# Attention stage of a three-stage kernel: row copies out of PSUM, and a small addition, moved from VectorE to ScalarE

## The chip, the cores and the metric

The kernel runs on one core of one Trainium2 chip. The metric is the device time of one execution in microseconds; the time of a kernel is the median of several runs. Five engines work side by side, each through its own list of instructions in order: TensorE (PE in the rows; PEld is its weight load), VectorE (DVE), ScalarE (ACT), GpSimd (POOL) and SyncE (SP), which issues most transfers. They wait for one another by semaphores. TensorE writes its results to PSUM, a small memory of eight banks, from which VectorE and ScalarE read.

## What is computed

Three stages follow one another. Attention runs over 4 batches, 8 heads, 576 positions and 64 dimensions, with a window of 32 keys (dilated by 4 in the upper four heads). Its output, as 2304 rows of 512, goes through a mixture of 8 experts of which each row uses the one with the largest gate, and then through a dense two-layer block. Cut to what the change touches:

```python
scores = where(mask, scale * q @ k.T, -1e9)
attn = exp(scores - max(scores)); attn = attn / (sum(attn) + 1e-9)
x = (attn @ v).transpose(0, 2, 1, 3).reshape(2304, 512)
logits = x @ w_gate + modality_bias[modality_id]
e_idx = argmax(logits)
probs = exp(logits - max(logits)); probs /= sum(probs) + 1e-9
out[row] = probs[row, e_idx] * (relu(x @ w1[e_idx]) @ w2[e_idx])
```

The dense block comes after that and is not touched.

## The kernel before

The attention stage handles 16 pairs (batch b, head pair hp), in two halves each: a half, called a unit, is 5 or 4 blocks of 64 queries. The function attention() writes out a software pipeline by hand, as a loop over steps s = 0 to 37. The instructions of an engine run in the order in which this loop writes them. In step s it writes, in this order:

- on even s, the score matmuls of the pair s/2 (L1178 the mask, L1188 the scores; both units of the pair);
- emit_max_exp of unit s: the row maximum nb on VectorE (L1195), its scaling on ScalarE (L1196), 5 or 4 exponentials on ScalarE (L1200), each with a sum into su, and the addition of 1e-9 to su on ScalarE (L1202);
- emit_norm of unit s-1: a reciprocal on VectorE (L1209), and the multiplication on GpSimd (L1210);
- emit_b of unit s-3: transposes on TensorE (L1217), and the copy pt out of PSUM on VectorE (L1219);
- one store of rows that an earlier step made ready (L1301, by SyncE);
- emit_rows, where a pair of rows is pending (below);
- emit_c of unit s-4: the product with v on TensorE (L1232) and, after the second half, the copy xy on ScalarE (L1238, or L1240 with a stride for the dilated heads);
- routing work for the experts, on VectorE for the most part (from step 14 on; lines 240 to 360), loads of expert weights, and, in steps 19, 21, 23, 25, 27, 29, 33 and 35, the split of a weight tile: a cast whi on ScalarE (L201), then wlo on GpSimd (L203).

emit_rows(b, c, t0) turns the finished columns of xy into rows. It takes up to three tiles of 128 rows: one matmul each against [identity, gate weights] (L1252) writes 128 row values and 8 gate logits to the PSUM bank ps_r, of which there is one. For the first three head pairs of a batch (c < 3), the rows are copied to xc (L1255) and the logits to lp (L1256), both on VectorE; xc goes to memory by a store. For the last head pair the logits are added up first (L1267), and the rows are copied to xe (L1272 on VectorE, for the last batch L1270 on ScalarE). The next call of emit_rows, one step later, writes the same bank again. The rows of a pair i are made in steps 2i+6 and 2i+7: batch 0 in steps 6 to 13, batch 1 in 14 to 21, batch 2 in 22 to 29, batch 3 in 30 to 37.

emit_gate runs once for each batch, after its last rows (steps 13, 21, 29 and 37): a maximum, a subtraction, an exponential on ScalarE (L1289), the position of the maximum, the sum sg (L1294), the addition of 1e-9 (L1295) and a reciprocal (L1296), all on VectorE but the exponential.

After step 37 the experts and the dense block follow; the expert work already starts in steps 28 to 36 (gathered rows: L626, L635, L637; first layer: L644, L654, L655).

Of the kernel before, what the change touches and what calls it, by code (L numbers as in the profile page):

```python
# [17 lines left out]
ACTF = mybir.ActivationFunctionType  # L18
ALU = mybir.AluOpType
# [1072 lines left out]
def attention(tc, qT, kT, vW, mod, w_gate, m_bias, cs, msk, xy, oh, tri16, one16, x_dram, banks, w, moe, rt):  # L1092
    nc = tc.nc
    ident = cs[:, C_ID:C_ID + 128]
    scale = 1.0 / float(D) ** 0.5
    with ExitStack() as st:
# [149 lines left out]
        def emit_rows(b, c, t0):  # L1246
            g = groups[b]
            n = min(3, g.stop - t0)
            o = t0 - g.start
            r = banks.r[:, 0:3 * 136].rearrange("p (t e) -> p t e", e=136)  # L1250
            for t in range(n):
                nc.tensor.matmul(r[:, t, :], xy[:, c, (t0 + t) * 128:(t0 + t + 1) * 128], rw[:, c, :], start=True, stop=True)  # L1252
            if c < HP - 1:
                xc = xc_p.tile([128, 3, 128], F32, tag="xc", name="xc")
                nc.vector.tensor_copy(xc[:, 0:n, :], r[:, 0:n, 0:128])  # L1255
                nc.vector.tensor_copy(lp[:, o:o + n, c, :], r[:, 0:n, 128:136])  # L1256
                stores.append((t0, n, c, xc[:, 0:n, :], 128))
                if c == HP - 2 and t0 + n == g.stop:
                    m = len(g)
                    nc.vector.tensor_reduce(ls[:, 0:m, :], lp[:, 0:m].rearrange("p t c e -> p t e c"), axis=AX.X, op=ALU.add)  # L1260
                    nc.vector.tensor_tensor(ls[:, 0:m, :], ls[:, 0:m, :], bm[:, g.start:g.stop, :], op=ALU.add)
                return
            if t0 == g.start:
                xe_t[b] = xe_p.tile([128, 5, 144], F32, tag="xe", name="xe")
                nc.vector.memset(xe_t[b][:, :, 129:144], 0.0)
            xe = xe_t[b]
            nc.vector.tensor_tensor(ls[:, o:o + n, :], ls[:, o:o + n, :], r[:, 0:n, 128:136], op=ALU.add)  # L1267
            last = t0 + n == g.stop
            if b == B - 1:
                nc.scalar.copy(xe[:, o:o + n, 0:128], r[:, 0:n, 0:128])  # L1270
            else:
                nc.vector.tensor_copy(xe[:, o:o + n, 0:128], r[:, 0:n, 0:128])  # L1272
            if last:
                xe_t.pop(b)
                emit_gate(b, xe)
                stores.append((g.start, len(g), c, xe[:, 0:len(g), :], 144))

        def emit_gate(b, xe):
            g = groups[b]
            n = len(g)  # L1280
            sl = slice(g.start, g.stop)
            l = ls[:, 0:n, :]
            x = sm.tile([128, 5, E], F32, tag="x", name="x")[:, 0:n, :]
            mx = sm.tile([128, 5], F32, tag="mx", name="mx")[:, 0:n]
            sg = sm.tile([128, 5], F32, tag="sg", name="sg")[:, 0:n]
            bc = [128, n, E]
            nc.vector.tensor_reduce(mx, l, axis=AX.X, op=ALU.max)
            nc.vector.tensor_tensor(l, l, mx.unsqueeze(2).to_broadcast(bc), op=ALU.subtract)
            nc.scalar.activation(x, l, ACTF.Exp)  # L1289
            rev = cs[:, C_REV:C_REV + E].unsqueeze(1).to_broadcast(bc)  # L1290
            nc.vector.scalar_tensor_tensor(l, l, 0.0, rev, op0=ALU.is_equal, op1=ALU.mult)
            nc.vector.tensor_reduce(mx, l, axis=AX.X, op=ALU.max)
            nc.vector.tensor_tensor(oh[:, sl, :], rev, mx.unsqueeze(2).to_broadcast(bc), op=ALU.is_equal)
            nc.vector.tensor_reduce(sg, x, axis=AX.X, op=ALU.add)  # L1294
            nc.vector.tensor_scalar(sg, sg, 1e-9, None, op0=ALU.add)  # L1295
            nc.vector.reciprocal(xe[:, 0:n, 128], sg)  # L1296

        def emit_store():
# [4 lines left out]
        for s in range(NU + 6):  # L1303
# [16 lines left out]
            if pend:  # L1320
                emit_rows(*pend.pop(0))
            if s == 28:
                next(ids)
            if 0 <= s - 4 < NU:
# [3 lines left out]
                if half == 1:  # L1328
# [3 lines left out]
                    b, hp = pairs[i]  # L1332
# [295 lines left out]
```

## Time and profile before

| | |
|---|---|
| time, median of 3 runs | 771.34 us (769.26 to 773.08) |
| the profiled execution | 769.39 us |
| its span in the trace | 767.6 us |
| TensorE busy | 739.3 us, 96% |
| VectorE busy | 491.3 us, 64% |
| ScalarE busy | 387.4 us, 50% |
| GpSimd busy | 99.3 us, 13% |

The attention stage fills the first 126 us or so of the span; the score matmuls of step 14 start at 46.02 us, those of step 16 at 52.06, of step 22 at 69.92, of step 30 at 98.30. Times in the rows are microseconds from the span's start. A row of the timeline gives start, duration, engine, line, operation, what it writes and reads, and, in brackets, how long the engine stood idle before it and which instruction ended that. Instructions of one engine overlap a little at their ends, so the next one may start some 0.1 us before the last has ended.

### The profile page before, as it was taken

To read this page: it belongs to the slowest core of one execution; us is meant where nothing else is said; L and a number is where in the kernel's file an instruction comes from. 1 tells how busy PE (TensorE), PEld (TensorE's weight loads), DVE (VectorE), ACT (ScalarE), POOL (GpSimd) and SP (SyncE) were. 2 spreads that over 40 slices of the span, in tenths; PEclk is the share of its full clock that TensorE was granted. 3 is DMA by queue.
4 is the path that set the end of the run, shared out by engine and by line. 5 is a ranking of instruction groups with operands and counts; after the bars stand their busy time and mean duration, and the time that the engine had idled before them with its cause. 6 is when DMAs were issued, how large, how long until landed. Compare 5 with 4: busy or idle time off the path is not lost. (4 is left out here: it accounts for less than half of the span.)

```text
span 767.6 us, 15236 instructions
## 1 busy us (share of the span) xinstructions
PE 739.3 (96%) x5537; PEld 658.5 (86%) x5539; DVE 491.3 (64%) x1149; ACT 387.4 (50%) x1008; POOL 99.3 (13%) x99
## 2 busy tenths in 40 slices
PE   8999879999999999999799999999999999999996
PEld 4888669988998899889799889888889888988895
DVE  3678886773887878986487777864444464344341
ACT  4878753223323323442376666775445566454453
POOL 3325542230110100000000000011000003000003
PEclk9999999999999999999999999999999999999999
DMA  7789951269898967932257777488544556455512
GB/s 205 201 234 296 268 174 44 59 186 331 292 324 275 336 193 253 318 115 75 80 183 286 275 266 284 164 298 304 192 151 163 219 219 227 159 198 216 190 55 82
DMA packets 66189, 161.05 MB, mean 210 GB/s; under 512 B 8416, under 2 KB 25824, under 8 KB 60080
## 3 DMA queue, kind: packets, MB, share of 16 engines
q1 hardware_dynamic: 62592, 148.58, 57.0%
q0 software_dynamic: 3360, 11.01, 4.3%
q8 instruction: 49, 0.80, 0.4%
q14 instruction: 44, 0.36, 0.1%
q10 hardware_dynamic: 144, 0.29, 0.1%
HBM read 118.82 MB, written 41.04 MB: 208 GB/s over the span
## 5 line engine op out<-in xcount | busy, mean ns | idle before, releaser
L1439 DVE SCALAR_TENSOR_TENSOR t<-x,t 128x384 f32<-128x384 f32 x92 | 51.4, 558 | 80.0 <-ACT t L1432 79.8
L1462 PE MATMUL d_o<-d_ob,gh 128*128 128x512 f32 x288 | 89.6, 392 | 0.0
L1462 PE MATMUL d_o<-d_plain,gh 128*128 128x512 f32 x288 | 89.6, 392 | 0.0
L644 PE MATMUL ps_e<-hh,whi 128*128 128x256 f32 x288 | 82.9, 288 | 2.0 <-PEq L668 0.9
L644 PE MATMUL ps_e<-hl,whi 128*128 128x256 f32 x288 | 81.1, 282 | 0.0
L644 PE MATMUL ps_e<-hh,wlo 128*128 128x256 f32 x288 | 81.1, 281 | 0.0
L1431 ACT ACTIVATE t<-x 128x384 f32<-128x384 f32 x92 | 48.3, 525 | 52.5 <-DVE x L1452 52.5
L1447 DVE TENSOR_TENSOR gl<-t,gh 128x384 fp32r<-128x384 f32 x96 | 53.2, 554 | 17.8 <-ACT gh L1440 15.7
L1440 ACT CAST gh<-t 128x384 fp32r<-128x384 f32 x96 | 49.4, 514 | 29.6 <-DVE t L1439 29.3
L1452 DVE TENSOR_TENSOR x<-d_y,d_u 128x384 f32<-128x384 f32 x46 | 25.5, 554 | 53.1 <-ACT d_u L1543 53.1
L1462 PEld LDWEIGHTS d_o<-d_plain,gh 128*128 128x128 f32 x288 | 52.9, 188 | 6.1
L1462 PEld LDWEIGHTS d_o<-d_ob,gh 128*128 128x128 f32 x288 | 52.8, 188 | 5.7
L644 PEld LDWEIGHTS ps_e<-hh,whi 128*128 128x128 f32 x288 | 54.5, 189 | 3.1 <-issue 2.3
L1462 PE MATMUL d_o<-d_ob,gl 128*128 128x512 f32 x144 | 57.2, 397 | 0.0
L1462 PE MATMUL d_o<-d_plain,gl 128*128 128x512 f32 x144 | 57.1, 396 | 0.0
L1543 ACT COPY d_u<-d_x 128x384 f32<-128x384 f32 x46 | 22.0, 479 | 65.1 <-PE d_x L1419 65.1
L644 PEld LDWEIGHTS ps_e<-hh,wlo 128*128 128x128 f32 x288 | 54.5, 189 | 0.0
L644 PEld LDWEIGHTS ps_e<-hl,whi 128*128 128x128 f32 x288 | 54.4, 189 | 0.0
L663 ACT COPY xy<-ps_e 128x256 f32 (+1 forms) x36 | 13.4, 373 | 79.6 <-PE ps_e L644 65.1
L1432 ACT ACTIVATE t<-t 128x384 f32<-128x384 f32 x96 | 50.5, 526 | 3.0
L1471 POOL DMA_INDIRECT out<-o,pid x18 | 17.9, 995 | 248.4 <-ACT o L1470 246.6
L1200 ACT ACTIVATE p<-ps_s,nb 128x96 f32<-128x96 f32 x144 | 47.1, 341 | 2.7 <-issue 0.4
(441 smaller groups left out, 1922.8 us busy)
## 6 DMA issues: line engine op xcount, KB each, us to landing
raw<-in_w SPq DMA_DIRECT2D x48, 512.0 KB, 7.1
d_ab<-cache SPq DMA_DIRECT2D x15, 1024.0 KB, 6.2
d_ab<-cache SPq DMA_DIRECT2D x15, 768.0 KB, 4.3
r<-in_w_in SPq DMA_DIRECT2D x16, 512.0 KB, 5.8
r<-in_w_out SPq DMA_DIRECT2D x16, 512.0 KB, 5.4
wsc<-cva SPq DMA_DIRECT2D x32, 256.0 KB, 4.2
cache<-d_ab SPq DMA_DIRECT2D x8, 1024.0 KB, 5.0
d_ob<-cache SPq DMA_DIRECT2D x8, 1024.0 KB, 7.5
```

The source lines that it names most:

```text
L644: self.tc.nc.tensor.matmul(ps, a, b, start=(i == 0 and j == 0), stop=(i == n - 1 and j == 2))
L663: nc.scalar.copy(self.xy[:, d, off], ps)
L1200: nc.scalar.activation(p[:, j, :], s[:, j, :], ACTF.Exp, scale=scale, bias=nb[:, j:j + 1], accum_out=su[:, j:j + 1])
L1431: nc.scalar.activation(b.t, x, ACTF.Relu, scale=0.5, bias=0.5)
L1432: nc.scalar.activation(b.t, b.t, ACTF.Square)
L1439: nc.vector.scalar_tensor_tensor(b.t, x, 1.0, b.t, op0=ALU.max, op1=ALU.min)
L1440: nc.scalar.copy(b.h, b.t)
L1447: nc.vector.tensor_tensor(b.l, b.t, b.h.bitcast(F32), op=sub)
L1452: nc.vector.tensor_tensor(x, bank, other, op=add)
L1462: nc.tensor.matmul(po[i], a[:, q], o[:, x, f, :], start=(first and j == 0), stop=(last and j == 2))
L1471: nc.gpsimd.indirect_dma_start(out=outs[n][:, :], out_offset=bass.IndirectOffsetOnAxis(ap=pid[:, n:n + 1], axis=0), in_=t, in_offset=None)
L1543: nc.scalar.copy(part[("p1", "u2", "u3")[j // 2]], bank)
```

## The change

The copy of the rows to xc goes to ScalarE for batches 1, 2 and 3, and stays on VectorE for batch 0. The copy of the logits to lp stays where it is. The addition of 1e-9 to the gate's sum goes from VectorE to ScalarE, as an activation with a bias, in all four batches.

```diff
@@ emit_rows
             if c < HP - 1:
                 xc = xc_p.tile([128, 3, 128], F32, tag="xc", name="xc")
-                nc.vector.tensor_copy(xc[:, 0:n, :], r[:, 0:n, 0:128])
+                (nc.vector.tensor_copy if b < 1 else nc.scalar.copy)(xc[:, 0:n, :], r[:, 0:n, 0:128])
                 nc.vector.tensor_copy(lp[:, o:o + n, c, :], r[:, 0:n, 128:136])
@@ emit_gate
             nc.vector.tensor_reduce(sg, x, axis=AX.X, op=ALU.add)
-            nc.vector.tensor_scalar(sg, sg, 1e-9, None, op0=ALU.add)
+            nc.scalar.activation(sg, sg, ACTF.Copy, bias=1e-9)
             nc.vector.reciprocal(xe[:, 0:n, 128], sg)
```

In all, 18 copies (two in each of nine pairs of steps: nine of 128x384, six of 128x256, three of 128x128) and four additions change engines. The instructions of TensorE, GpSimd and SyncE stand in the same order as before.

On ScalarE, in step 16, the copy stands behind the exponentials and the su addition of unit 16 and ahead of the scaling of unit 17 (in brackets: the engines and transfer queues that an instruction waits for):

```order
 L1200 ACTIVATE p,su<-ps_s_82,nb 128x96 x4
 L1202 ACTIVATE su<-su 128x5 [waits Activation_49]
+L1255 COPY xc<-ps_r 128x384 [waits DMAHW1_49,DMAHW0_49,PE_49]
 L1196 ACTIVATE nb<-nb 128x4 [waits DVE_49]
-L1200 ACTIVATE p,su<-ps_s_83,nb 128x96 [waits PE_49,Activation_49,Pool_49]
+L1200 ACTIVATE p,su<-ps_s_83,nb 128x96 [waits Activation_49,Pool_49]
 L1200 ACTIVATE p,su<-ps_s_83,nb 128x96 x3
```

One instruction came in; the rest kept its order.

On VectorE, in the same step, between the maximum of unit 16 (L1195) and the routing work (L302, L303), with the reciprocal of unit 15 (L1209) and the pt copy of unit 13 (L1219):

```order
 L300 CAST ri<-rt_sm 1x1 [waits DVE_49]
 L1195 TENSOR_REDUCE nb<-ps_s_82 128x5 [waits PE_49]
-L1209 RECIPROCAL su<-su 128x4 [waits Activation_49,Pool_49]
+L1209 RECIPROCAL su<-su 128x4 [waits Pool_49]
 L1219 COPY pt<-ps_t 96x512 [waits PE_49]
-L1255 COPY xc<-ps_r 128x384 [waits DMAHW0_49,PE_49]
-L1256 COPY lp<-ps_r 128x3x8
+L1256 COPY lp<-ps_r 128x3x8 [waits Activation_49]
 L302 TENSOR_SCALAR rt_key<-cs,rt_r_138 128x8
 L303 TENSOR_SCALAR rt_k_143<-rt_key 128x8 [waits DVE_49]
```

The xc copy left the list, the lp copy got a wait for ScalarE, and the reciprocal lost one.

On ScalarE, in step 21, between the gate's exponential (L1289) and the xy copy of that step (L1238), with the weight cast (L201) behind it:

```order
 L1202 ACTIVATE su<-su 128x4 [waits Activation_49]
 L1289 ACTIVATE x<-ls 128x40 [waits DVE_49]
+L1295 ACTIVATE sg<-sg 128x5 [waits DVE_49]
 L1238 COPY xy<-ps_o 128x576 [waits PE_49]
 L201 CAST whi_97<-raw 128x1024 [waits DMAHW4_49]
```

The addition came in between, with a wait for VectorE.

## Rows read from the trace of the kernel before

**Rows 1.** The page's first part: busy time of each engine.

```profile
PE 739.3 (96%) x5537; PEld 658.5 (86%) x5539; DVE 491.3 (64%) x1149; ACT 387.4 (50%) x1008; POOL 99.3 (13%) x99
```

**Rows 2.** Windows: length; busy PE, PEld, DVE, ACT, POOL; clock; DMA share; GB/s.

```profile
46.02:57.98 11.96, 11.96 (x192) 10.21 (x191) 10.40 (x43) 8.81 (x47) 3.82 (x5) 1.00 0.84 237
...
81.58:98.30 16.72, 12.17 (x193) 10.14 (x192) 14.17 (x42) 11.54 (x49) 9.14 (x8) 1.00 0.79 231
...
110.00:126.00 16.00, 15.93 (x183) 15.02 (x182) 10.11 (x36) 7.61 (x13) 6.15 (x3) 1.00 0.38 112
```

**Rows 3.** Timeline of steps 16 and 17, three engines.

```profile
52.06 1.75 PE L1188 MATMUL ps_s<-k,q 64*64 64x96 f32 x36
...
53.85 0.66 DVE L1195 TENSOR_REDUCE nb<-ps_s 128x5 f32<-128x480 f32 x1 [0.28 <-PE ps_s L1188]
...
54.55 0.21 ACT L1196 ACTIVATE nb<-nb 128x5 f32<-128x5 f32 x1 [0.89 <-DVE nb L1195]
...
55.12 0.56 DVE L1255 COPY xc<-ps_r 128x384 f32<-128x384 f32 x1
...
55.60 0.17 DVE L1256 COPY lp<-ps_r 128x24 f32<-128x24 f32 x1
...
56.34 0.63 PE L1252 MATMUL ps_r<-rw,xy 128*128 128x136 f32 x4
...
56.49 0.55 DVE L1195 TENSOR_REDUCE nb<-ps_s 128x4 f32<-128x384 f32 x1
56.59 0.21 ACT L1202 ACTIVATE su<-su 128x5 f32<-128x5 f32 x1
...
57.08 0.20 ACT L1196 ACTIVATE nb<-nb 128x4 f32<-128x4 f32 x1 [0.28 <-DVE nb L1195]
...
58.09 0.16 DVE L1256 COPY lp<-ps_r 128x16 f32<-128x16 f32 x1
...
58.79 0.17 DVE L253 TENSOR_TENSOR rt_lo<-rt_rank,rt_tmp 128x4 f32<-128x4 f32 x1
58.80 0.20 ACT L1202 ACTIVATE su<-su 128x4 f32<-128x4 f32 x1
...
59.77 0.66 DVE L1195 TENSOR_REDUCE nb<-ps_s 128x5 f32<-128x480 f32 x1 [0.82 <-PE ps_s L1188]
```

**Rows 4.** Timeline of steps 36 and 37: the xe copies on ScalarE.

```profile
123.23 0.48 ACT L1270 COPY xe<-ps_r 128x384 f32<-128x384 f32 x1 [0.61 <-DVE ls L1267]
...
124.95 0.37 ACT L1270 COPY xe<-ps_r 128x256 f32<-128x256 f32 x1 [0.57 <-DVE ls L1267]
```

**Rows 5.** Timeline of steps 21 and 22: the gate's sum, and the next scaling.

```profile
71.59 0.19 DVE L1294 TENSOR_REDUCE sg<-x 128x5 f32<-128x40 f32 x1
...
72.78 0.21 ACT L1196 ACTIVATE nb<-nb 128x5 f32<-128x5 f32 x1 [0.33 <-DVE nb L1195]
```

**Rows 6.** Timeline of steps 24 to 28.

```profile
77.53 0.66 DVE L1195 TENSOR_REDUCE nb<-ps_s 128x5 f32<-128x480 f32 x1
...
79.51 1.86 DVE L327 TENSOR_TENSOR rt_v<-oh,rt_isM 128x72 f32<-128x72 bf16 x1
...
86.97 0.20 ACT L1196 ACTIVATE nb<-nb 128x5 f32<-128x5 f32 x1
...
94.03 0.20 ACT L1196 ACTIVATE nb<-nb 128x5 f32<-128x5 f32 x1
```

**Rows 7.** Timeline of steps 29 to 32, from the gate's addition on.

```profile
102.17 2.10 DVE L1295 TENSOR_SCALAR sg<-sg 128x4 f32<-128x4 f32 x1
...
105.06 0.21 ACT L1196 ACTIVATE nb<-nb 128x5 f32<-128x5 f32 x1 [3.26 <-DVE nb L1195]
...
105.83 1.27 PE L1217 MATMUL ps_t<-cs,p 128*96 128x128 f32 x5 [3.23 <-DVE pt L1219]
...
109.17 0.66 PE L635 MATMUL ps_s<-cs,xga 128*128 128x128 f32 x4
```

**Rows 8.** Windows, columns as in rows 2: the stretch behind that gap.

```profile
105.00:107.50 2.50, 1.67 (x8) 1.66 (x9) 1.79 (x7) 2.24 (x14) 0.83 (x1) 0.63 0.55 165
```

## The prediction

> **What bounds the kernel now.** I read the page's first part, then the table of windows over the attention stage, then the timeline of one pair of steps. TensorE is busy for 96% of the span [rows 1], so only time that TensorE loses can lengthen the run, and only time that it loses today can be won. The change touches nothing after 126 us. From 46.02 to 57.98 us TensorE has no gap at all (11.96 of 11.96 us) at a full clock, while VectorE works 10.40 and ScalarE 8.81 us; from 81.58 to 98.30 us it stands for 4.55 us [rows 2]. So the copies leave a VectorE that does not set the pace in the first stretch, and may do so in the second.
>
> The pace of two steps (16 and 17) is in [rows 3]. TensorE ends the scores at 53.81 us (52.06 + 1.75), VectorE's maximum starts at 53.85, ScalarE's scaling of it at 54.55, five exponentials follow, and the small su add starts at 56.59. Beside this, VectorE copies xc at 55.12 and lp at 55.60, and TensorE starts the second row matmuls at 56.34, into the bank that both copies have just read. That is 0.25 us before ScalarE even starts its su add. The copies are done in the shade of the exponentials. The next pair's maximum starts at 59.77, so a pair takes 5.92 us.
>
> **Part 1: 18 copies go to ScalarE.** On VectorE one of 128x384 takes 0.56 us [rows 3]. On ScalarE the same shape out of the same bank (the xe copy of the last batch) takes 0.48 us and 128x256 takes 0.37 us [rows 4]; for 128x128 no row stands, and the same slope gives an estimate of 0.27 us. The size of the work is a draw. The place is not: on ScalarE the copy stands behind the step's exponentials and su, and the maximum of the next step stands behind nothing but VectorE's own order.
>
> The second thing is the lp copy, which stays on VectorE. The order of the changed program, printed with the change above, gives it a wait for ScalarE, where before it had none; that is, VectorE may read the bank only when ScalarE has read it. The last batch's rows show that such a wait is real: its xe copy on ScalarE stood idle 0.61 and 0.57 us until VectorE's read of the same bank (L1267) was over [rows 4]. Behind lp on VectorE, in order, are the routing work, the next step's maximum, its reciprocal and the pt copy. So ScalarE's next exponentials wait for a maximum that waits for lp, that waits for xc, that waits for the last exponentials. Two engines that overlapped now take turns.
>
> The Trainium skill speaks of this: "PSUM — Partial Sum Buffer", section "PSUM bank collisions raise a hardware error", says that ScalarE and VectorE may not read one bank at the same time, so that software has to order them. By that rule lp must wait, and the trace agrees in [rows 4]; without it the sum would be the first rival's.
>
> The new length of the pair 16/17, from [rows 3], each term a difference of starts: maximum to scaling 0.70 (53.85 to 54.55); scaling to su 2.04 (to 56.59); su to lp 0.64 (0.11 to the next instruction, an estimate from starts of neighbours of this size, the copy's 0.48, and 0.05 for the signal, as between 54.51, the end of the maximum, and 54.55); lp to the odd maximum 0.89 (55.60 to 56.49, routing included); maximum to scaling 0.59 (to 57.08); scaling to su 1.72 (to 58.80); su to lp 0.53 (the copy now 0.37); lp and its routing 0.87 (58.09 to 58.96). Sum 7.98 us against 5.92: **2.06 us more**. The other way round, through TensorE: 0.70 + 2.04 + 0.64 + 0.22 (lp and a signal, then the row matmuls) + 3.43 (56.34 to 59.77) = 7.03, which is shorter, so VectorE and ScalarE taking turns set the pace. TensorE then stands for some 2 us of each pair. Three pairs (steps 14 to 19, batch 1) are of this form. The last has one product of 128x256 where 16/17 has four small routing steps, and I take 0.4 us off for it, an estimate: 2.06 + 2.06 + 1.7 = **5.8 us**. Bounds: 1.1 each if routing were free (7.03), so 3.3; and 6.5 at most.
>
> Batch 2 (steps 22 to 27). Pair 22/23 is of the same form: **2.0 us**. From 24 on the trace has waits of its own, which take up part. The pair 24/25 lasts 9.44 us today (maximum at 77.53, scaling of step 26 at 86.97), because a product of 128x72 takes 1.86 us on VectorE [rows 6] while GpSimd works. Retimed with the terms above, with 1.4 us for lp to the odd maximum (the routing without that stall) and 2.2 us from the odd su to the scaling of step 26 (2.02 today, 0.17 for xc), it is 0.70 + 2.04 + 0.64 + 1.4 + 0.58 + 1.72 + 2.2 = 9.3: **0**. If the product is held up as before, it is +1.9. Pair 26/27: today 7.06 us between scalings (86.97 to 94.03); new 2.04 + 0.64 + 0.9 + 0.58 + 1.72 + 2.2 = 8.1: **1.0 us**.
>
> Batch 3. Pair 30/31 is the same again: from its scaling, 2.05 + 0.64 + 0.09 + 0.58 + 1.71 + 0.53 + 0.53 = 6.13 to the transposes of the gathered rows (L635), against 4.11 today (105.06 to 109.17 [rows 7]): **2.0 us**. Steps 32 to 35 have no exponentials, ScalarE waits for TensorE there and TensorE is busy for 15.93 of 16.00 us [rows 2]: their four copies cost 0, and the cover is ScalarE's own idle time (7.61 of 16.00 us busy).
>
> **Part 2: the 1e-9.** Four times ScalarE takes one instruction of some 0.2 us between the gate's exponential and the xy copy. It waits for VectorE's sum (L1294), and behind it stand xy, the weight cast and the next step's scaling, and TensorE's row matmuls wait for xy. In step 21 that sum ends at 71.78, so xy starts at 71.94 and not 70.88; the cast follows, and the scaling of step 22, at 72.78 today [rows 5], comes at 73.41: **0.6 us** more. In step 13 it is 0.1 at most, an estimate: no cast stands behind it there, and ScalarE waits for the next maximum anyway. In step 37 it is 0 to 0.2: the following first-layer result waits, TensorE hardly. In step 29 it is a gain: there the same add takes 2.10 us on VectorE [rows 7], while GpSimd works, and the maximum of step 30 waits behind it. Started at 102.17 on ScalarE it would be over by 102.39 (0.2 us, as the su adds), xy and the cast done by 103.76, and the scaling of step 30 comes then and not at 105.06: **-1.3 us**. Bounds: 0 if another VectorE instruction is held up in its place, -1.5 more if TensorE's gap of 3.23 us [rows 7], after which the granted clock was 0.63 [rows 8], is short enough to keep the clock.
>
> **Sum.** 5.8 + 2.0 + 0 + 1.0 + 2.0 + 0.1 + 0.6 - 1.3 + 0.1 = 10.3 us; stepping through the stage end to end, with what each delay shifts, I come to 10.9, and take 10.7. What follows the stage is a chain that starts from its end, so all of it arrives. The profiled execution took 769.39 us: 780.1. The median of the runs shown is 771.34, 1.95 more, and the measurement is of medians: **782 us**. Bounds from the terms: 3.3 + 1 + 0 + 0.5 + 0.5 - 2.8 = 2.5 below and 6.5 + 2.6 + 1.9 + 1.5 + 2.5 + 1 = 16 above, so 774 to 787.
>
> **Rivals.** First, **lp does not matter** and only TensorE's bank is late: the second row matmuls wait 0.9 us in the pairs up to 23, by the TensorE path without lp, and steps 24 to 31 hide theirs in gaps that are there already. Then 4 x 0.9 + 0.6 - 0.5 = +3.7, 775 us. For it: VectorE has slack (10.40 of 11.96 us). Against it: the order's wait, and [rows 4].
>
> Second, **the relief of VectorE wins**. From 81.58 to 98.30 us VectorE works 14.17 of 16.72 us and TensorE stands for 4.55 [rows 2]. Six copies between steps 24 and 31 (2.6 us) and the add of 2.10 us go. If ScalarE copied at once, up to 4 us of TensorE's gaps would close: 767 us. It decides if xc starts within half a microsecond of its matmuls; it cannot while five exponentials, 2 us, stand ahead. The Trainium skill, "TensorEngine Tiling (Array Packing)", section "PSUM Bottleneck", advises to use both ScalarE and VectorE to empty PSUM; by that rule this rival is the one. The trace has both at it already (xy and pt), and this copy's bank is read by both.
>
> Third, **it does little**: part 2's gain in step 29, with a clock that holds, meets a loop at the lower bound: within 3.9 us of before.
>
> Fourth, **the clock falls**: gaps of 2 us in six pairs bring what the gap of 3.23 us brought, a granted clock of 0.63 [rows 8]. TensorE's 3.4 us from the row matmuls to the next maximum then take some 2 us more in six pairs, +12 on top: 794 us. Against it: between 81.58 and 98.30 us, with gaps in it, the clock stayed at 1.00 [rows 2].
>
> **How the numbers follow.** The forecast has 0.68; lp without weight 0.11; little 0.08; relief 0.05; clock 0.08. Half a per cent, 3.9 us, is about what a measurement of this kernel can tell from no change. Slower by more: the forecast, the clock and half of the first rival, 0.82; faster 0.04; the rest, 0.14, the same. The range runs from 774.5 (the first rival in it) to 788, a microsecond past the upper bound.
>
> **What would show it.** Right, if after shows VectorE idle before lp until ScalarE's xc, some 0.6 to 1.5 us each, if pairs 14 to 19 take 7.5 to 8 us each, and if TensorE's second row matmuls wait for lp. Part 2 is right if step 29's gate has no 2 us instruction and step 21's xy comes about 1 us later. Wrong, if lp follows xc without idle time, or if the stage from 126 us on starts less than 6 us later than before.

## The result, and the profile after

The changed kernel took **782.73 us** (median of 4 runs, 782.43 to 782.79) beside 771.51 us for the kernel before (4 runs, 769.26 to 773.08): a ratio of 1.0149, with an interval of 1.0132 to 1.0166, or 11.2 us more. The forecast was 782. The profiled execution took 782.43 us with a span of 780.6 us.

The first row of the page of after, which answers to [rows 1]:

```profile
PE 747.4 (96%) x5539; PEld 663.5 (85%) x5539; DVE 479.1 (61%) x1127; ACT 394.3 (51%) x1030; POOL 98.7 (13%) x99
```

VectorE works 12.2 us less and ScalarE 6.9 us more, so on both engines together there is less to do than before, and the run is longer. TensorE is busy 8.1 us longer with the same products; part of them ran at a lower clock (below). Where the loss begins is seen in the waits. Three groups of the waits of after (who waited on which line, for whom: us in total, times, the longest):

```profile
DVE lp L1256 <- ACT xc L1255: 26.2, 15, 2.6
...
PE ps_r L1252 <- DVE lp L1256: 6.7, 6, 1.4
...
ACT sg L1295 <- DVE sg L1294: 4.3, 4, 1.8
```

The first did not exist before: there both copies were VectorE's own. Now lp stands idle for ScalarE's xc 15 times, 26.2 us in all, and six times TensorE's next row products wait for lp in turn. Steps 16 and 17 in the timeline of after (start, duration, what; idle time before it and its releaser in brackets), to be laid beside [rows 3]:

```profile
56.08 0.64 DVE L1195 TENSOR_REDUCE nb<-ps_s 128x5 f32<-128x480 f32 x1
...
56.75 0.21 ACT L1196 ACTIVATE nb<-nb 128x5 f32<-128x5 f32 x1 [1.41 <-DVE nb L1195]
...
58.79 0.21 ACT L1202 ACTIVATE su<-su 128x5 f32<-128x5 f32 x1
58.90 0.46 ACT L1255 COPY xc<-ps_r 128x384 f32<-128x384 f32 x1
...
59.40 0.18 DVE L1256 COPY lp<-ps_r 128x24 f32<-128x24 f32 x1 [2.02 <-ACT xc L1255]
...
59.63 0.73 PE L1252 MATMUL ps_r<-rw,xy 128*128 128x136 f32 x4 [1.39 <-DVE lp L1256]
...
60.30 0.55 DVE L1195 TENSOR_REDUCE nb<-ps_s 128x4 f32<-128x384 f32 x1
...
60.89 0.20 ACT L1196 ACTIVATE nb<-nb 128x4 f32<-128x4 f32 x1 [1.52 <-DVE nb L1195]
...
62.73 0.35 ACT L1255 COPY xc<-ps_r 128x256 f32<-128x256 f32 x1
...
63.12 0.17 DVE L1256 COPY lp<-ps_r 128x16 f32<-128x16 f32 x1 [1.47 <-ACT xc L1255]
63.91 0.65 DVE L1195 TENSOR_REDUCE nb<-ps_s 128x5 f32<-128x480 f32 x1
...
64.60 0.21 ACT L1196 ACTIVATE nb<-nb 128x5 f32<-128x5 f32 x1 [0.42 <-DVE nb L1195]
```

Read the brackets from the top down. ScalarE waits 1.41 us for VectorE's maximum; VectorE's lp waits 2.02 us for ScalarE's xc; TensorE waits 1.39 us for lp; ScalarE waits 1.52 us for the next maximum, which stands behind lp on VectorE; lp waits 1.47 us again. The two engines take turns. From scaling to scaling (56.75 to 64.60) the pair takes 7.85 us, against 5.92 us in the kernel before (54.55 to 60.47). In these two stretches TensorE stands idle for 1.95 us in after and not at all in the kernel before. The copies themselves take 0.46 and 0.35 us, less than on VectorE (0.56 and 0.41 us).

The even steps' scalings and the transposes behind them, before and after, give the loss stretch by stretch. (Each number is the growth of the distance between the same two rows in the two traces. Together they make up the 13.0 us between the two profiled executions; the medians are 11.2 us apart.)

| stretch | forecast, us | measured, us |
|---|---|---|
| steps 14/15 | 2.06 | 2.16 |
| steps 16/17 | 2.06 | 1.93 |
| steps 18/19 | 1.7 | 1.69 |
| steps 20/21, with the gate of step 21 | 0.6 | 0.74 |
| steps 22/23 | 2.0 | 1.79 |
| steps 24/25 | 0 | 0.30 |
| steps 26/27 | 1.0 | 0.96 |
| steps 28/29, with the gate of step 29 | -1.3 | -1.29 |
| steps 30/31, to the first transposes (L635) | 2.0 | 2.08 |
| steps 32 to 35 | 0 | 1.44 |
| behind the attention stage | 0 | 1.2 |

Both gate terms are visible. In step 29 the addition is ScalarE's, waits 1.84 us for VectorE's sum and takes 0.21 us, where VectorE took 2.10 us in [rows 7]; TensorE then waits for xy behind it. The gate and the row products behind it, in the timelines of after:

```profile
111.59 0.18 DVE L1294 TENSOR_REDUCE sg<-x 128x4 f32<-128x32 f32 x1
111.81 0.21 ACT L1295 ACTIVATE sg<-sg 128x4 f32<-128x4 f32 x1 [1.84 <-DVE sg L1294]
111.92 0.62 ACT L1238 COPY xy<-ps_o 128x576 f32<-128x576 f32 x1
...
112.59 1.73 PE L1252 MATMUL ps_r<-rw,xy 128*128 128x136 f32 x6 [2.33 <-ACT xy L1238]
```

The last two terms of the table are in the main the clock's. The windows of after behind that gap of 2.33 us (columns as in [rows 2]; the clock is the third number from the end):

```profile
110.00:112.50 2.50, 0.26 (x3) 0.01 (x1) 2.16 (x6) 0.69 (x3) 1.15 (x2) 0.97 0.88 320
112.50:115.00 2.50, 2.41 (x20) 2.16 (x22) 0.92 (x3) 2.42 (x12) 1.44 (x1) 0.50 0.41 128
...
120.00:122.50 2.50, 2.50 (x14) 2.46 (x12) 1.16 (x3) 0.59 (x1) 0.21 (x1) 0.50 0.88 278
122.50:125.00 2.50, 2.50 (x35) 2.21 (x34) 0.60 (x3) 1.06 (x2) 0.61 (x1) 0.99 0.67 216
```

For ten microseconds TensorE has half its clock, the lower of its two levels (1.2 GHz). While something else sets the pace no loss shows (steps 30/31 came out at 2.08 us, 2.0 forecast), but steps 32 to 35 are TensorE's own, and the second transposes come 3.89 us after the first (119.57 and 123.46), where in the kernel before it is 2.45 us (109.17 and 111.62). At the start of the last stage the lower clock comes in both kernels, and lasts longer in after: in its first ten microseconds the granted clock is 0.62 and 0.69 in two windows of 5 us, against 0.66 and 1.00 in the kernel before, and the distance between the two traces grows by 0.9 us; the remaining 0.3 us come in small steps before that.

### The profile page after: what moved, and what is told of

Same layout as the page of the kernel before. It is cut to its first block, busy times and chain, and to the rows that moved or that the text cites. A ratio compares the mean times of both kernels' runs of the same rounds, so it can differ in the third digit from the quotient of the medians.

```text
span 780.6 us, 15226 instructions
## 1 busy us (share of the span) xinstructions
PE 747.4 (96%) x5539; PEld 663.5 (85%) x5539; DVE 479.1 (61%) x1127; ACT 394.3 (51%) x1030; POOL 98.7 (13%) x99
```

## The experiments

The medians of the kernel before differ by up to 1 us from one set of runs to the next (771.19 to 772.23); every ratio is against the runs beside it.

### One part alone

**e1: part 1 alone.** The edit:

```diff
-                nc.vector.tensor_copy(xc[:, 0:n, :], r[:, 0:n, 0:128])
+                (nc.vector.tensor_copy if b < 1 else nc.scalar.copy)(xc[:, 0:n, :], r[:, 0:n, 0:128])
```

> Part 1 of the change alone: the 18 copies on ScalarE, the 1e-9 on VectorE as before. Turn-taking theory (lp waits for xc, and VectorE's next maximum stands behind lp): nearly the whole change, 11 to 12 us over before, 782 to 783.5 us; the pairs of steps 14 to 19 last 7.5 to 8 us each. If part 2 carried much of it, it would be 3 us or more below the full change. Also told: whether step 29's gate has its add of about 2 us on VectorE again; if yes the scaling of step 30 comes some 1.3 us later than in the full change.

Measured: 783.42 us, ratio 1.0152 (1.0134 to 1.0170). The wait of lp for xc is there 15 times again. The gate's addition in step 29 is back on VectorE, with its old length:

```profile
111.80 2.10 DVE L1295 TENSOR_SCALAR sg<-sg 128x4 f32<-128x4 f32 x1
```

The scaling of step 30 comes 1.3 us later than in the changed kernel, as expected. The whole loss belongs to the copies.

**e2: part 2 alone.** The edit:

```diff
-            nc.vector.tensor_scalar(sg, sg, 1e-9, None, op0=ALU.add)
+            nc.scalar.activation(sg, sg, ACTF.Copy, bias=1e-9)
```

> Part 2 alone: the four additions of 1e-9 on ScalarE, all copies on VectorE. By the terms of the prediction: +0.1 (step 13), +0.6 (step 21), -1.3 (step 29, to the scaling of step 30), up to 0.2 (step 37): -0.5 us, 771.0 us, ratio 0.9993; up to 1.5 us less if the clock does not fall behind step 29. If the additions were a cost by themselves (ScalarE blocked for about 1 us in four steps), it would be +2 to +4 us.

Measured: 771.49 us, ratio 1.0004 (0.9991 to 1.0016): no difference. The 2.10 us are gone from VectorE, but on TensorE they come back at another place. Before, it waited 3.23 us for pt behind the late maximum; now it waits 2.33 us for xy, which stands behind the addition on ScalarE:

```profile
104.52 0.21 ACT L1295 ACTIVATE sg<-sg 128x4 f32<-128x4 f32 x1 [1.84 <-DVE sg L1294]
104.63 0.62 ACT L1238 COPY xy<-ps_o 128x576 f32<-128x576 f32 x1
...
105.30 0.96 PE L1252 MATMUL ps_r<-rw,xy 128*128 128x136 f32 x6 [2.33 <-ACT xy L1238]
```

By the distances between rows, step 29 gains 1.3 us; the price is 0.5 us in steps 14/15 (behind the gate of step 13), 0.6 at the gate of step 21, 0.4 in steps 22/23 and 0.5 from the scaling of step 30 to the first transposes. Behind the new gap the clock is at 0.50 too.

### Is it the place, or the engine?

**e3: lp ahead of xc.** The changed kernel with the two copies in the other order, so that xc waits for lp and not lp for xc:

```diff
-                (nc.vector.tensor_copy if b < 1 else nc.scalar.copy)(xc[:, 0:n, :], r[:, 0:n, 0:128])
                 nc.vector.tensor_copy(lp[:, o:o + n, c, :], r[:, 0:n, 128:136])
+                (nc.vector.tensor_copy if b < 1 else nc.scalar.copy)(xc[:, 0:n, :], r[:, 0:n, 0:128])
```

> The full change with two lines swapped: VectorE reads the logits (lp) first, ScalarE's xc copy follows it. So lp no longer waits for ScalarE, and what is left of the cost is TensorE's bank, which comes free only behind the exponentials. Turn-taking theory: most of the cost goes; a pair of steps lasts 0.70 + 2.04 + 0.59 + 0.05 + 3.43 = 6.8 us by TensorE's path and not 8; in all about +4 us, 775 to 776 us, ratio 1.005. If the cost were the late bank alone, or ScalarE's added work, the swap would change nothing: 782 to 783 us.

Measured: 776.0 us, ratio 1.0061 (1.0039 to 1.0082): 6.7 us less than with the change, by the swap of two lines. Steps 16 and 17 in its timeline (lp is L1255 here, xc L1256):

```profile
56.60 0.18 DVE L1255 COPY lp<-ps_r 128x24 f32<-128x24 f32 x1
57.58 0.55 DVE L1195 TENSOR_REDUCE nb<-ps_s 128x4 f32<-128x384 f32 x1
58.00 0.21 ACT L1202 ACTIVATE su<-su 128x5 f32<-128x5 f32 x1
58.11 0.46 ACT L1256 COPY xc<-ps_r 128x384 f32<-128x384 f32 x1
...
58.62 0.73 PE L1252 MATMUL ps_r<-rw,xy 128*128 128x136 f32 x4 [0.72 <-ACT xc L1256]
```

Here lp waits for nothing, and the next maximum is done before ScalarE needs it. What is left is TensorE's path: it waits for xc, which still stands behind the exponentials, and a pair takes 6.90 us (scores at 60.37 and 67.27). This is the first rival, made true by an edit, and it gives the time that the rival gave (775). So of the 11.2 us some 6.7 hang on lp's turn behind xc, and some 4.5 are left. The 6.7 hold the 1.44 us of steps 32 to 35, which e3 does not lose (its transposes stand 2.45 us apart, 112.97 and 115.42); in what is left, the pairs of steps lose 4.7 us in the trace by the bank that TensorE gets back late, and the gates of steps 21 and 29 give back 0.9.

**e7: xc ahead of the exponentials.** Part 1 alone, with the copy written ahead of the exponentials of its step. The core of the edit (the function that issues a step's softmax stops once, behind the maximum, and is resumed behind emit_rows):

```diff
             nc.vector.tensor_reduce(nb[:, 0:n], s[:, 0:n, :], axis=AX.X, op=ALU.max)
+            yield
             nc.scalar.activation(nb[:, 0:n], nb[:, 0:n], ACTF.Copy, scale=-scale)
...
-                emit_max_exp(s)
+                exps = emit_max_exp(s)
+                next(exps)
...
+            if s < NU:
+                next(exps, None)
```

> All copies from the second batch on are on ScalarE, as in the changed kernel, but written ahead of the five exponentials of their step (maximum and scaling first, then the row products and the copy, then the exponentials). The 1e-9 stays on VectorE. If the place behind the exponentials is what costs, xc starts within 0.2 us of its row products, lp's waits fall from 26.2 us to under 10, and the exponentials, some 0.7 us late, are taken up where ScalarE has idle time, not in steps with a weight cast: about 774.5 us, 772 to 776. If it is ScalarE's added work, or that two engines read the bank at all, it stays at 782.

The edit stops ahead of the scaling, not behind it as the expectation says: the scaling, too, now stands behind the copy, and in a gate's step the gate's exponential stands ahead of it.

Measured: 776.25 us, ratio 1.0062 (1.0039 to 1.0084). lp's waits fell to 8.2 us, as expected, and the loss to less than half, 0.25 us above the expected range of 772 to 776. Part of the price is at the new place:

```profile
57.55 0.48 ACT L1256 COPY xc<-ps_r 128x384 f32<-128x384 f32 x1 [1.05 <-PE ps_r L1253]
57.93 0.21 ACT L1197 ACTIVATE nb<-nb 128x5 f32<-128x5 f32 x1
58.06 0.18 DVE L1257 COPY lp<-ps_r 128x24 f32<-128x24 f32 x1 [0.64 <-ACT xc L1256]
```

Now ScalarE waits 1.05 us for the row products, with the scaling and five exponentials behind it. Over the six pairs of steps 14 to 19 and 22 to 27 the trace is 2.8 us longer than that of the kernel before. Steps 12/13 and 20/21, which have no xc on ScalarE, are 4.0 us longer: there ScalarE waits 1.61 and 2.10 us for the gate with the scaling and the exponentials behind it. ScalarE's work is the same as in e1; some 6 us of difference (11.4 and 5.1 us over the kernel before) are position. Of the three places that were tried on ScalarE, none costs nothing; the one between the scaling and the exponentials was not tried.

### Do the terms add up?

**e5: the second batch alone.** `nc.scalar.copy if b == 1 else nc.vector.tensor_copy` for xc, nothing else.

> Only the copies of the second batch (steps 14 to 21, the six of the pairs 14 to 19) are on ScalarE; the 1e-9 stays on VectorE. If the forecast's terms may be added, this costs what the three pairs cost there: the maximum of step 20 comes 5.8 us later than before, all of it arrives at the end, and the time is 772.0 + 5.8 = 777.8 us, 777 to 778.5. If later waits take up part of a delay (the rival), it is under 776; if the loss needs all the batches (the clock, say), under 774.

Measured: 777.54 us, ratio 1.0072 (1.0048 to 1.0096), 6.35 us more for 5.8 forecast. The three pairs took 7.66, 8.62 and 7.72 us from scaling to scaling, against 5.78, 5.92 and 6.01 before. The middle one is 0.8 us longer than the same pair in after, and the lower clock falls into it (0.71 from 60 to 65 us), as it does in e1 (8.55 us, 0.66). All of the delay arrived at the end.

**e6: steps 32 to 35 alone.** `nc.scalar.copy if b == 3 and c > 0 else nc.vector.tensor_copy`, four copies.

> Only the four copies of steps 32 to 35, which have no exponentials, are on ScalarE. The forecast's term for them is 0: 772.0 us, within 0.5. In the changed kernel these steps ran 1.44 us longer than before, at a granted clock of 0.50. If the copies themselves cost that, by the order of the readers, it shows here as 773.4 us; if the clock cost it, it does not show.

Measured: 771.53 us, ratio 1.0001 (0.9986 to 1.0016). Within the interval (some 1.2 us either way) the copies cost nothing there: the term of 0 was right for them, and the 1.44 us have another cause. Here too the profiled execution had a clock of 0.50 in this stretch, with the two transposes 4.37 us apart (109.00 and 113.37), and this without a loss in the median. So the stretch may vary by up to 2 us from run to run; that it does so in the kernel before is not shown, as there is one trace of it.

### The clock

**e8: both gaps filled.** The changed kernel, with products of zeros in place of TensorE's idle time ahead of step 30's row products and of the first transposes:

```diff
             if pend:
+                warm(8 if s == 30 else 0, (banks.s[2],))
                 emit_rows(*pend.pop(0))
...
             if s in (31, 32):
+                warm(8 if s == 31 else 0, (banks.s[2],))
                 moe.tx(0, s - 31, banks.s[(2, 0)[s - 31]])
```

> The changed kernel with eight products of zeros on TensorE in each of two gaps: ahead of the row products of step 30 (a gap of 2.33 us, after which the granted clock was 0.50 for 10 us) and ahead of the first transposes of the gathered rows in step 31. Nothing reads what they write, and no engine waits for them. If the gap brought the clock down, and the clock brought the 1.44 us that steps 32 to 35 lost, then the clock stays at 1.00 from 112 to 122 us, the second transposes come 2.5 us after the first and not 3.9, and the time is 781.3 us. If the clock falls for another reason, or the steps were long for another, it stays at 782.7.

Measured: 778.93 us, ratio 1.0100 (1.0078 to 1.0121). The granted clock is 1.00 in every window from 90 to 122.5 us, and the two transposes stand 2.45 us apart (120.27 and 122.72). So the gap brought the clock down, and the clock brought the 1.44 us. But the time fell by 3.8 us, and the theory explains 1.4.

**e9: the first gap alone filled.** The first of the two added lines.

> The changed kernel with eight products of zeros on TensorE in the first of the two gaps alone, ahead of the row products of step 30; nothing reads them. With both gaps filled the clock stayed at 1.00, the second transposes came 2.45 us after the first, and the time fell by 3.8 us and not by the 1.4 expected. If the gap of 2.33 us alone brought the clock down, it stays at 1.00 here too from 112 to 122 us, and the two transposes stand 2.45 us apart; the time is then 781.3 us by what the trace of the changed kernel shows, or 779 if the rest of the 3.8 us hangs on the clock or on the added products as well.

Measured: 780.88 us, ratio 1.0120 (1.0102 to 1.0138). The clock held from 112 to 120 us, then fell behind the next gap, against what was expected:

```profile
121.21 0.66 PE L635 MATMUL ps_s<-cs,xga 128*128 128x128 f32 x4 [1.94 <-DVE xga L626]
...
122.14 1.55 PE L1252 MATMUL ps_r<-rw,xy 128*128 128x136 f32 x6
```

The row products of 122.14 take 1.55 us where 0.86 us is their length at full clock, and the transposes are 3.68 us apart. Two microseconds less by the median all the same: most of that is not the clock of this stretch.

**e10: the kernel before with its gap filled.** 14 such products ahead of step 31's transposes, in the 3.23 us of [rows 7].

> The kernel before with 14 products of zeros on TensorE in its gap of 3.23 us ahead of step 31's transposes, after which its granted clock was 0.63 to 0.69 for 5 us. Nothing reads them. If the clock follows the gap, it stays at 1.00 from 105 to 110 us. The row that ends this stretch in the profile, VectorE's scaling of the gathered rows, came no earlier at a full clock (3.33 us after the transposes against 3.34), so the time stays at 771.2 us; if runs differ by a clock that falls lower in some (0.50 in the run with the tail's copies, where the two transposes stood 4.37 us apart and not 2.45), it is up to 1.9 us less, 769.3.

Measured: 766.71 us, ratio 0.9940 (0.9924 to 0.9956). The clock stayed at 1.00 behind the filled gap as expected, but a gain of 5.0 us was in neither expectation. In the trace the attention stage ends no earlier (first transposes at 109.70); 3.2 us go near 380 us, where the last stage begins and this edit has no work at all. 2.1 of them go at the first product there (e12 below), and 0.9 behind it, where the clock is 1.00 (378.9 to 383.9 us) and was 0.66 in the kernel before (381 to 386).

**e12: 24 instructions more, no gap filled.** The search for that gain. In the kernel before, the program's first twelve products of zeros are written as 24 of half the width: the same columns at the same place, 24 instructions more on TensorE.

```diff
-        warm(12, (banks.r, banks.s[1], banks.s[2]))
+        for i in range(24):
+            h = 256 * (i // 3 % 2)
+            nc.tensor.matmul((banks.r, banks.s[1], banks.s[2])[i % 3][:, h:h + 256], wz[:, 0:128], wz[:, 0:256], start=True, stop=True)
```

> The kernel before with the first 12 products of zeros of the program (128x512, from 1.2 us on) written as 24 of 128x256: the same columns in the same place, 24 instructions more on TensorE, no gap filled. In the three kernels with filled gaps or one gap filled, and in the fourth, the first product of the last stage (near 380 us) came 0.10 us after the cast that it waits for; in nine kernels whose TensorE program has 5555 instructions it came 0.96 to 2.96 us after. If the number of instructions ahead does it (where TensorE's code is cut for loading), it comes 0.1 us after the cast here too and the time is 2.1 us less, some 769.3 us. If it was the filled gap, through the clock, it comes 2 us after and the time stays at 771.5.

Measured: 767.52 us, ratio 0.9936 (0.9918 to 0.9953). No gap is filled, the clock is 0.50 behind the gap of 3.22 us, and the gain is there: 4.7 us, where 2.1 were expected. The place that the traces show is the first product of the last stage. In the kernel before, the cast that makes its operand, the last that it needs, ends at 379.21, and the product comes 2.23 us later:

```profile
378.85 0.36 DVE L1400 CAST d_B110h<-xy 128x384 fp32r<-128x384 f32 x1 [3.71 <-DVEq L139]
...
381.44 0.58 PE L1419 MATMUL d_x<-d_B110h,d_plain 128*128 128x384 f32 x2 [3.77 <-DMA d_wo<-wsc]
```

In e12, where two lines more stand ahead in the code, it comes 0.10 us later:

```profile
380.21 0.36 DVE L1402 CAST d_B110h<-xy 128x384 fp32r<-128x384 f32 x1 [3.62 <-DVEq L139]
...
380.67 0.59 PE L1421 MATMUL d_x<-d_B110h,d_plain 128*128 128x384 f32 x2 [1.56 <-DVE d_B110h L1402]
```

The releaser that the first row names cannot be meant: in e10 the product started 0.62 us after the issue of that transfer, too early for it to have landed (the two issued there landed 2.8 and 4.7 us after their issue). Over all traces: with TensorE's program unchanged in number (before, after, e1 to e7; 5537 to 5539 products on their pages) the product comes 0.96 to 2.96 us after the cast; with 16 to 32 instructions more (e8 to e12) 0.10 or 0.11 us. In e8 and e9 that is 0.9 us less than in after, a part of what the clock did not explain there. The page's rows of transfers split the same way. Before, after and e1 to e7 have the first of these rows, e8 to e12 the second:

```profile
q8 instruction: 49, 0.80, 0.4%
```

```profile
q8 instruction: 48, 0.79, 0.4%
```

One transfer of code less is made. This points to the loading of code at this place as what the added instructions move; it is inferred, not seen. The Trainium skill, "Runtime: NRT & Kernel Launch", section "Instruction fetch mechanics", says that an engine's code comes in blocks of 256 instructions and that a jump to code outside the loaded blocks waits for it. The trace agrees in that the number of instructions ahead decides and that the count of transfers changes; no row shows TensorE waiting for a block by name.

### What beats both kernels

**e4: the addition behind the step's copies.** The kernel before with the addition on ScalarE, but it and the reciprocal issued at the end of the step, behind xy and the weight cast (a list holds them until then):

```diff
-            nc.vector.tensor_scalar(sg, sg, 1e-9, None, op0=ALU.add)
-            nc.vector.reciprocal(xe[:, 0:n, 128], sg)
+            late_gate.append((xe, n, sg))
+
+        def emit_gate_end():
+            while late_gate:
+                xe, n, sg = late_gate.pop(0)
+                nc.scalar.activation(sg, sg, ACTF.Copy, bias=1e-9)
+                nc.vector.reciprocal(xe[:, 0:n, 128], sg)
```

> Before with part 2 alone, but the addition and the reciprocal are written at the end of the step, so on ScalarE the addition stands behind the xy copy and the weight cast. Theory: xy keeps its place, so the loss of step 21 (0.6 us) goes, and TensorE's gap behind the gate of step 29, 3.2 us in before, falls under 2 us, so that the clock stays up: the scaling of step 30 some 1.9 us earlier than in before, in all -1.5 to -3.5 us, 768 to 770 us, ratio 0.9955 to 0.998. If another VectorE instruction is held up in place of the add of 2.10 us: no change.

Measured: 767.85 us, ratio 0.9959 (0.9943 to 0.9975). The addition's wait for the sum now stands behind xy, and TensorE's waits here are 0.28 and 1.33 us, with a third of 1.52 us ahead of the first transposes; the clock is 1.00 from 100 to 115 us:

```profile
99.62 0.62 ACT L1238 COPY xy<-ps_o 128x576 f32<-128x576 f32 x1
...
100.29 0.96 PE L1252 MATMUL ps_r<-rw,xy 128*128 128x136 f32 x6 [0.28 <-ACT xy L1238]
...
101.55 0.21 ACT L1300 ACTIVATE sg<-sg 128x4 f32<-128x4 f32 x1 [0.36 <-DVE sg L1294]
...
103.31 0.72 PE L1217 MATMUL ps_t<-cs,p 128*96 128x128 f32 x5 [1.33 <-DVE pt L1219]
```

The trace places 1.9 us of the gain in step 29. The scaling of step 22 still comes 0.6 us late, against what was expected, but by step 24 this is made up. The medians are 4.2 us apart (0.15 us below the expected 768 to 770); the trace does not place the rest.

**e11: e4 with its two gaps filled.** Six products of zeros ahead of step 31's transposes and six ahead of the first transposes of gathered rows.

> The kernel with the 1e-9 and the reciprocal behind the step's xy and weight cast (767.85 us), with six products of zeros in each of its two gaps of 1.33 and 1.52 us in step 31. Its clock was at 1.00 there without them, so the theory expects no change, 767.9 us, within 1; if such products bring something by themselves, as the surplus of 2.4 us with both gaps filled would have it, it is 765 to 766.

Measured: 763.58 us, ratio 0.9904 (0.9884 to 0.9923), the fastest of all and below both expectations. The clock theory, applied to these two gaps, expected no change and was wrong; the products do bring something by themselves, and e12 says what: they are 24 instructions, and the last stage's first product stands 0.10 us behind its cast here too, at 377.46 us against 378.93 in e4, though the rows ahead of it came 0.97 us later than in e4. Behind it another 1.2 us go: the clock is 1.00 there (377.4 to 382.4 us) and was 0.66 in e4 (378.9 to 383.9).

## Why the prediction was right

**The mechanism** was the one forecast: VectorE's lp waits for ScalarE's xc, and both copies' engines take turns. e1 and e3 show it from both sides. The pairs 14 to 19 take 7.94, 7.85 and 7.70 us, inside the 7.5 to 8 that were to show it; lp's waits are longer than the 0.6 to 1.5 us that were named (26.2 us in 15, 1.7 on average). **The terms** of steps 14 to 31 sum up to 10.1 us in the forecast and measure 10.4; none is off by more than 0.3 us. The retimed pair 16/17 was 2.06 us longer by the working, 1.93 by the trace. The zero for steps 24 and 25 was right for its stated reason too: the product of 128x72, 1.86 us in [rows 6], takes 0.25 us at its new time.

```profile
89.84 0.25 DVE L327 TENSOR_TENSOR rt_v<-oh,rt_isM 128x72 f32<-128x72 bf16 x1
```

**Part 2's terms** were +0.6 in step 21 (0.74 measured), -1.3 in step 29 (-1.29). What the forecast did not carry on from the second is that the gain makes a wait of TensorE for xy, 2.33 us, in place of the one removed. In e2 that is one reason why part 2 alone is worth nothing. The other is step 13: the forecast gave it 0.1 us at most, and in e2 steps 14/15 behind it are 0.5 us longer.

**A term that was mis-sized:** steps 32 to 35. The forecast gave their four copies 0 with TensorE busy as their cover. For the copies that is right (e6). But it took TensorE at its full clock there, and by the rows it had the lower one: 1.44 us. The fourth rival, the falling clock, had the cause and the wrong place and size: it priced gaps of 2 us in all six pairs with 12 us. In after the pairs' gaps, 0.9 to 1.4 us of waiting for lp, left the clock at 1.00 with one exception (0.50 from 92.5 to 95 us, where the loss stayed at 0.30 us); one gap of 2.33 us did not. In e1 and e5 the exception is the pair 16/17, at a price of 0.7 to 0.8 us.

**Two errors that cancel.** The profiled execution was forecast at 780.1 us and took 782.43; the median was put 1.95 us above the profiled one, as in the kernel before, and was 0.30 above it. The first error is the clock of steps 32 to 35 and of the last stage's start. The second is that the profiled run of the kernel before was one of its fastest; runs of it differ by 4 us, and e6, e10 and e12 point to two places where they may: the clock behind the gap of 3.23 us, and the first product of the last stage. The traces show a third, at the start: ahead of step 2 after and e1 to e11 have the same instructions as the kernel before, yet the scaling of step 2 stands between 0.64 us earlier (e4) and 1.76 us later (e9) than there; in e9 TensorE waits 1.74 us there for the load of k. That the median was met to 0.7 us is in part luck.

**The other rivals.** "lp does not matter" gave 775 us, and an edit that makes it so (e3) gave 776.0: its working was right, its condition was not met. The relief of VectorE did not come: VectorE has 12.2 us less to do, and nothing of it arrives.

What stays open: of the 4.7 us that e12 gains by the medians, the pair of traces at hand places 2.1 us at the first product; before is there with one of its fastest runs and e12 with its slowest, so the two traces can't place the rest (e12's also waits 1.66 us for k near the start, which before does not). And the 0.63 of [rows 8] is a mean over both levels: in finer windows the clock behind the gap of 3.2 us is 0.50 in the kernel before (105.7 to 109.0 us) and in e12 (105.2 to 111.9 us) alike. Why it lasts longer in one than in the other is not settled.

## What to carry to other kernels

Before a copy out of PSUM is moved to another engine, look at what else reads the same bank, and who stands behind each reader: here two readers on one engine needed no signal, two readers on two engines waited for each other, and the wait landed on whatever is queued behind the second (here the next maximum; swapping two lines was worth 6.7 us of 11). Moving a small instruction onto a shared queue pays, here, only behind what others wait for: the same addition was worth nothing ahead of the xy copy (e2), and the run was 3.6 us shorter with it behind (e4). And when an edit gains or loses near 0.5% far from where it works, see first whether it changed the number of instructions ahead of that place.

## What the runs showed of the hardware

- **Single gaps brought TensorE's clock to its lower level.** Between 40 and 130 us all ten gaps of 1.94 to 3.23 us in these fourteen traces were followed by a granted clock of 0.50, for up to 10 us (2.33 us in after and e2, 1.94 us in e9, 3.22 us in e12). Shorter gaps went both ways. Two gaps close together, of 0.6 to 0.8 and 1.5 us, brought it in e2, e4, e5, e6, e7, e10 and e12 (0.67 and 0.65 in e4's windows from 85 to 90 us) and not in the kernel before or e11; the gap of 1.39 us in the pair 16/17 brought it in e1 and e5 and not in after, e8 or e9. What decides between them is not settled. Products of zeros that nothing reads kept the clock at 1.00 in the gaps that they filled (e8, e10).
- **24 more TensorE instructions, with the same columns computed, were worth 4.7 us** (767.52 against 772.23), 2.1 of them in the traces at one product. What fits the runs is that they move the point where code is loaded. Comparing two kernels with different counts, one may measure this too.
- **Some small VectorE instructions last until GpSimd's is over.** In e1 the addition on 128x4 (111.80 us, 2.10 us long) ends at 113.90, and GpSimd's splitting of a weight block, under which it runs, ends at 113.87:

```profile
111.51 2.36 POOL L203 TENSOR_TENSOR wlo<-raw,whi 128x1024 fp32r<-128x1024 f32 x1 [0.35 <-ACT whi L201]
```

The product of 128x72 took 1.86 us in [rows 6] and 0.25 us in after, where it comes after such an instruction is over (at 89.22 us) and not under it. So for these two the start, and not the size, set the duration. It is not so for all: under the GpSimd instruction of 78.92 to 81.28 us in the kernel before, the lp copy took its usual 0.17 us, and the product of 128x72 that followed it lasted until 81.37.
